# One core: the first batch's attention heads multiply P with v in 64 columns, and their x has one half

## The chip, the cores and the metric

The kernel runs on one core of one Trainium2 chip. The metric is the device time of one execution in microseconds (us), lower is better. Before the change it is 1084.87 us, the median of three runs (1084.13 to 1085.30).

## The reference, cut to what matters

Four batches of eight attention heads (sequence 576, head dimension 64, a mask of 64-row blocks) give x; x passes a dense layer pair with a product, and then a router and eight experts of which each token uses two.

```python
scores = scale * np.matmul(q, k.transpose(0, 1, 3, 2))     # 4 x 8 heads, 576 x 576
attn = np.exp(scores - max); attn = attn / (sum + 1e-09)    # after the mask
x = np.matmul(attn, v)                                       # -> (2304, 512)
a, b = x @ w1, x @ w2
x = (a * b @ w3) @ w_out
...                                                          # router, top 2 of 8 experts
out[mask] += w * (np.maximum(x[mask] @ w1[e], 0.0) @ w2[e])
```

## The kernel before, in words

**Precision.** Products that need more than one pass split a float32 operand into a rounded high part and a low remainder (`split`, L473 to 481: ScalarE writes the high part, VectorE or GpSimd subtracts). `mm3` (L483 to 488) then issues three matmuls, high by high, high by low, low by high. Every expert and dense product goes through L486, L487, L488.

**Attention, heads 8 to 31.** The transposed probabilities P and v are split. The stationary operand `vv` (L619 to 625) is 128 columns wide: 64 of the high part of v, 64 of the low part. P's two parts are multiplied with it in two matmuls. The result has 128 rows, two halves of 64 whose sum is the head's output. Both halves are written to the DRAM tensor `x2[head, 128, 576]` and added later.

**Attention, heads 0 to 7 (the first batch).** P and v stay plain float32, one matmul per piece (the trace shows two records for each). v is loaded into columns 0 to 63 of a 128-column tile `vz` (two tiles, filled with zeros once at L590 to 593, loaded at L600 to 605). So rows 64 to 127 of the result are zeros. They are copied out of PSUM, written to `x2`, read back and added like the others.

**Matmul pieces of one head.** `av_a` (L685) multiplies the last piece, 128 columns of P, into a bank of the pool `tp`, and VectorE copies it into `ev` (L692). `av_b` (L694) does five pieces of 448, 448, 320, 192 and 128 columns in two steps, three pieces and then two. ScalarE copies the result into `ev` (L705), and the SyncE (SP) queue writes `ev` to `x2` (L706).

**The dense layers.** x is consumed in nine chunks of 256 tokens (`Moe1.steps`). Chunks 0 and 1 lie in the first batch (tokens 0 to 511); of chunk 2, 64 tokens do; chunks 3 to 8 need none of it. For a chunk, `x_load` reads both halves of `x2` into `x.ab` and the reciprocal row sums into `x.r`, all on SP. `x_prep` has three steps: GpSimd adds the two halves (L191), VectorE multiplies by the reciprocal sums (L194), and `split` gives the two parts `xh` (L477, L481). Chunk 0 is taken in two parts of three and one tile (heads 0 to 5, then 6 and 7), the others in one.

**The order of work.** Each attention head is a list of short operations written out by hand (`FIRST` for heads up to 9, `LATER` after). `f2.9` in it lets a generator put about 2.9 us of other TensorE work there: first the product of w3 and w_out (`w_unit`, L722), then the dense layers. `c` feeds the conversion of weights: 1024-column pieces come as 64-bit integers (L540), VectorE turns them into float32 in three passes (L549, L550, L551) and `split` makes the parts `pc` (L477, L481). An `ahead` step places `x_load` and the three steps of `x_prep`. When the program is built, each engine's final order is made from these lists, their priorities and a simulated timeline. Each engine then works its own list in order, and SP issues almost every plain DMA, also in order.

**Names in the rows.** `sb` are banks of scores (L644 to 647), `pb` is exp (L663), `tp` L677 the transposes of P, `pt` P transposed (L681, L683), `av` L702 and `tp` L690 the products of P and v, `hi` and `kl` the parts of q and k (L612 to 617), `stg` and `stf` raw and converted weights, `pc` their parts, `m<-xh` the dense products, L711 a transpose of the sums with 40 columns.

Of the kernel before, what the change touches and what calls it, by code (L numbers as in the profile page):

```python
# [8 lines left out]
F32 = mybir.dt.float32  # L9
# [5 lines left out]
OP = mybir.AluOpType  # L15
# [4 lines left out]
B, H, S, D = 4, 8, 576, 64  # L20
NT, DM, DF, E = 2304, 512, 1024, 8
BH = B * H
P = 128
# [6 lines left out]
CH = 256  # L30
# [17 lines left out]
AV0 = 1280  # L48
# [33 lines left out]
class Moe1:  # L82
# [72 lines left out]
    def x_load(self, c):  # L155
        nc, k, p2 = self.nc, self.k, self.p2
        x = self.xs[c] = Ctx()
        x.ab = self.p2b.tile([P, 4, 2, CH], F32, name="xab")
        x.r = self.p2b.tile([P, 4, CH], F32, name="xr")
        t0, o = c * CH, 0  # L160
        while o < CH:
            b, s = divmod(t0 + o, S)
            n = min(CH - o, S - s)
            for g, e in self.parts(c):
                for hh in range(2):
                    hs = slice(hh * 64, (hh + 1) * 64)
                    for ab in range(2):
                        d = nc.sync.dma_start(x.ab[hs, g:e, ab, o:o + n],
                                              k.x2[b * H + 2 * g:b * H + 2 * e, ab * 64:(ab + 1) * 64, s:s + n]
                                              .rearrange("(t q) d s -> q d t s", q=2)[hh])  # L170
                        for h in range(b * H + 2 * e, (b + 1) * H):
                            self.tc.declare_no_dep(d.ins, k.x2w[h].ins, reason="another head")
                    nc.sync.dma_start(x.r[hs, g:e, o:o + n],
                                      k.rs[b, 2 * g:2 * e, s:s + n].rearrange("(t q) s -> q t s", q=2)[hh:hh + 1]
                                      .broadcast_to([64, e - g, n]))
            o += n
        if ZC <= c < ZC + 4:
            with self.tc.issue_after(d.ins):
                self.setup_dram(c - ZC + 1)
# [6 lines left out]
    def x_prep(self, c, step):  # L186
        nc, p2 = self.nc, self.p2
        x = self.xs[c]
        if step == 0:
            for g, e in self.parts(c):  # L190
                nc.gpsimd.tensor_tensor(x.ab[:, g:e, 0, :], x.ab[:, g:e, 0, :], x.ab[:, g:e, 1, :], op=OP.add)  # L191
        elif step == 1:
            for g, e in self.parts(c):
                nc.vector.tensor_tensor(x.r[:, g:e, :], x.ab[:, g:e, 0, :], x.r[:, g:e, :], op=OP.mult)  # L194
        else:
            x.h = self.p2b.tile([P, 2, 4, CH], F32R, name="xh")
            for g, e in self.parts(c):
                self.k.split((x.h[:, 0, g:e], x.h[:, 1, g:e]), x.r[:, g:e, :])
# [266 lines left out]
class Kernel:  # L465
# [89 lines left out]
    def attention(self):  # L555
        tc, nc, a = self.tc, self.nc, self.a
        moe1 = self.moe1
        stgs = ExitStack()
        with tc.tile_pool(name="p1", bufs=1, side="right") as p1, \
# [15 lines left out]
            px = moe1.px = pxs.enter_context(tc.tile_pool(name="px", bufs=1))  # L575

            def buf(h, shape, dt, name):

                return (px if h < H and h % 2 else p1).tile(shape, dt, name=name)
# [7 lines left out]

            vz = []  # L590
            for h in range(2):
                vz.append(px.tile([P, 5, P], F32, name=f"vz{h}"))
                nc.gpsimd.memset(vz[h], 0.0)

            def load(h):
                c = hd[h] = Ctx()
                c.qk = buf(h, [P, 2, S], F32, "qk")
                nc.sync.dma_start(c.qk, a["qk"][h])

            def load_v(h):  # L600
                c = hd[h]
                if h < H:
                    c.vv = vz[h % 2]
                    nc.sync.dma_start(c.vv[:, :, 0:D], a["v"][h])
                    return
                c.v = p1.tile([P, 5, D], F32, name="v")
                nc.sync.dma_start(c.v, a["v"][h])
# [77 lines left out]
            def av_a(h):  # L685
                c = hd[h]
                bank = psT.tile([P, 512], F32, name="tp")
                m = c.pt.shape[1]
                for i in range(m):
                    nc.tensor.matmul(bank[:, 0:P], c.vv[:, 0, :], c.pt[:, i, AV0:AV0 + P], start=(i == 0), stop=(i == m - 1))  # L690
                c.ev = buf(h, [P, S], F32, "ev")
                nc.vector.tensor_copy(c.ev[:, 0:128], bank[:, 0:128])  # L692

            def av_b(h, kts):  # L694
                c = hd[h]
                if kts[0] == 0:
                    c.av = psV.tile([P, 512], F32, name="av")
                for kt in kts:
                    _, s0, w, o0 = AV_UNITS[kt]
                    m = c.pt.shape[1]  # L700
                    for i in range(m):
                        nc.tensor.matmul(c.av[:, o0:o0 + w], c.vv[:, kt, :], c.pt[:, i, s0:s0 + w],  # L702
                                         start=(kt == 0 and i == 0), stop=(kt == 4 and i == m - 1))
                if kts[-1] == 4:
                    nc.scalar.copy(c.ev[:, 128:576], c.av[:, 0:448])  # L705
                    self.x2w[h] = nc.sync.dma_start(self.x2[h], c.ev)  # L706

            def sums_out(b):
                sp = psT.tile([P, 512], F32, name="tp")
# [113 lines left out]
            prep_h(0)  # L823
            load(1)
            load_v(0)
            feed()
            feed()

            def step(i, j, op):
# [4 lines left out]
                elif kind == "c":  # L834
                    feed()
                elif kind == "t":
                    tick()
                elif kind == "g" and i >= 0:
                    g_unit(i, int(n))
                elif kind == "p" and i >= 0:  # L840
                    prep_v(i)
                elif kind == "a" and i >= 0:
                    av_a(i)
                elif kind == "b" and i >= 0:
                    av_b(i, [0, 1, 2] if n == "0" else [3, 4])
                elif kind == "s" and j < BH:
                    s_unit(j, int(n))
                    s_max(j)
                elif kind == "h" and j + 1 < BH:
                    prep_h(j + 1)  # L850
                elif kind == "v" and 0 < j < BH:
                    load_v(j)
                elif kind == "l" and j + 2 < BH:
                    load(j + 2)
                elif kind == "o":
                    if i == H - 1 or i > H and i % H == 0:
                        sums_out((i - 1) // H if i > H else 0)
                    if i >= H:
                        moe1.ready = i // H
                    if i == 12:  # L860
                        assert not moe1.scat
                        with tc.issue_after(self.x2w[i - 1].ins):
                            moe1.setup_dram(0)
# [259 lines left out]
```

## Time and profile before

| | |
|---|---|
| Median of three runs | 1084.87 us (1084.13 to 1085.30) |
| The profiled execution | 1085.58 us |
| Its span, first to last instruction | 1083.8 us |
| Granted TensorE clock, mean | 0.987 of 2.4 GHz |
| TensorE matmul / VectorE / ScalarE / GpSimd busy | 1041.4 / 563.9 / 495.2 / 302.8 us |
| Attention of the first batch | about 10 to 110 us |
| Attention of the other batches, with the dense layers between | about 110 to 462 us |
| Dense layers' end and the experts | to 1083.8 us |

PE is TensorE's matmul side, PEld its weight loads, DVE VectorE, ACT ScalarE, POOL GpSimd, SP SyncE's queue. In a timeline row the first number is the start in us from the span's start, the second the stretch of time that the merged instructions cover, and what stands in brackets is how long the engine had been idle and what released it. Matmuls overlap in the pipe, so the distance from one start to the next tells what a matmul costs, not the length of its record. In a table by stretch each engine has its busy us and its number of instructions, then the granted clock, the share of time that the DMA engines were busy, and GB/s.

### The profile page before, as it was taken

The numbers are of one execution on the slowest core, as the hardware profiler recorded it, in microseconds if no ns is written. First come the engines' busy times: TensorE is split into PE (matmuls) and PEld (weight loads), VectorE is DVE, ScalarE is ACT, GpSimd is POOL, SyncE is SP. The second block draws the span as 40 slices with busy tenths as digits, with TensorE's granted clock in tenths as the row PEclk, the third lists the DMA queues.
The fourth block names the chain that finished last, engine by engine and source line by source line (L and its number), as shares of the span: only waits on it lengthen the run. The fifth ranks groups of instructions, "written<-read, shape, count | busy, mean of one in ns | idle before, by whom it ended". The sixth has DMA issues, their size and how long they took to land.

```text
span 1083.8 us, 17396 instructions
## 1 busy us (share of the span) xinstructions
PE 1041.4 (96%) x6588; PEld 941.8 (87%) x6588; DVE 563.9 (52%) x1211; ACT 495.2 (46%) x1163; POOL 302.8 (28%) x306
## 2 busy tenths in 40 slices
PE   6999887999999999999999999999999999999996
PEld 4777776899998989999999889889898989999885
DVE  7988898676764757443345443533333333434110
ACT  6875466566665666422223432533333333434111
POOL 2000233225252424332444224241413132220211
PEclk9999898999999999999999999999999999999998
DMA  8764878235653363222413355663535445351312
GB/s 269 255 225 152 222 206 170 82 108 134 184 118 104 122 186 98 78 80 59 79 45 114 98 125 170 183 158 98 153 101 147 108 129 125 108 117 31 39 20 32
DMA packets 78962, 136.34 MB, mean 126 GB/s; under 512 B 21165, under 2 KB 46485, under 8 KB 77717
## 3 DMA queue, kind: packets, MB, share of 16 engines
q1 hardware_dynamic: 68757, 113.98, 35.9%
q0 software_dynamic: 10112, 21.16, 10.7%
q8 instruction: 54, 0.88, 0.3%
q14 instruction: 39, 0.32, 0.1%
HBM read 103.92 MB, written 31.19 MB: 125 GB/s over the span
## 4 chain that ended last, share of the span: by engine, by line
PE 78%; DVE 3%; DMA 2%; ACT 1%; issue 1%; SPq 0%; POOL 0%; POOLq 0%; ACTq 0%; DVEq 0%
PE ph L486 13%; PE ph L488 13%; PE ph L487 13%; PE m L486 9%; PE m L487 9%; PE m L488 9%; PE tp L677 3%; PE av L702 3%; PE sb L647 1%; PE sb L644 1%; PE m L955 1%; DMA stf<-in_m_dram 1%; DMA yt<-cst 1%; PE m L244 1%; DVE pc L481 1%; PE m L235 1%
## 5 line engine op out<-in xcount | busy, mean ns | idle before, releaser
L486 PE MATMUL m<-xh,pc 128*128 128x256 f32 x576 | 166.9, 292 | 4.3 <-DVE pc L481 3.0
L487 PE MATMUL m<-xh,pc 128*128 128x256 f32 x576 | 163.7, 288 | 0.0
L488 PE MATMUL m<-xh,pc 128*128 128x256 f32 x576 | 162.3, 288 | 0.4 <-DVE pc L481 0.3
L486 PE MATMUL ph<-xt,pc 128*128 128x384 f32 (+1 forms) x512 | 156.1, 308 | 3.5 <-DVE ht L970 1.9
L487 PE MATMUL ph<-xt,pc 128*128 128x384 f32 (+1 forms) x512 | 157.1, 307 | 0.0
L488 PE MATMUL ph<-xt,pc 128*128 128x384 f32 (+1 forms) x512 | 156.9, 307 | 0.0
L970 DVE SCALAR_TENSOR_TENSOR ht<-ph,ht 128x384 fp32r<-128x384 f32 (+1 forms) x128 | 62.0, 490 | 148.8 <-ACT ht L969 142.9
L481 DVE TENSOR_TENSOR pc<-stf,pc 128x1024 fp32r<-128x1024 f32 (+1 forms) x75 | 88.1, 1190 | 87.9 <-ACT pc L477 83.8
L486 PE MATMUL ph<-pc,ht 128*128 128x512 f32 x320 | 126.0, 395 | 0.0
L488 PE MATMUL ph<-pc,ht 128*128 128x512 f32 x320 | 124.6, 390 | 0.0
L487 PE MATMUL ph<-pc,ht 128*128 128x512 f32 x320 | 124.5, 390 | 0.0
L997 POOL DMA_INDIRECT out_dram<-yo,ids x40 | 66.1, 1651 | 209.1 <-ACT yo L993 107.9
L969 ACT ACTIVATE ht<-ph 128x384 fp32r<-128x384 f32 (+1 forms) x128 | 55.1, 438 | 135.0 <-PE ph L488 132.5
L486 PEld LDWEIGHTS m<-xh,pc 128*128 128x128 f32 x576 | 111.3, 194 | 5.6 <-DVE pc L481 3.2
L487 PEld LDWEIGHTS m<-xh,pc 128*128 128x128 f32 x576 | 110.9, 194 | 0.8 <-DVE xh L481 0.2
L481 POOL TENSOR_TENSOR gt<-at,gt 128x256 fp32r<-128x256 f32 x72 | 59.2, 826 | 187.2 <-ACT gt L477 168.9
L488 PEld LDWEIGHTS m<-xh,pc 128*128 128x128 f32 x576 | 110.3, 194 | 1.0 <-DVE pc L481 0.8
L663 ACT ACTIVATE pb<-sb,nm 128x320 f32<-128x320 f32 (+3 forms) x192 | 93.7, 498 | 23.3 <-PE tp L677 15.5
L486 PEld LDWEIGHTS ph<-xt,pc 128*128 128x128 f32 x512 | 95.8, 188 | 4.5 <-DVE ht L970 2.1
L477 ACT CAST pc<-stf 128x1024 fp32r<-128x1024 f32 (+1 forms) x75 | 74.8, 1016 | 54.0 <-DMA stf<-in_m_dram 32.8
L487 PEld LDWEIGHTS ph<-xt,pc 128*128 128x128 f32 x512 | 96.1, 188 | 0.5 <-DVE xt L481 0.2
L488 PEld LDWEIGHTS ph<-xt,pc 128*128 128x128 f32 x512 | 96.2, 188 | 0.0
(159 smaller groups left out, 2164.4 us busy)
## 6 DMA issues: line engine op xcount, KB each, us to landing
stf<-in_m_dram SPq DMA_DIRECT2D x52, 512.0 KB
qk<-in_qk_dram SPq DMA_DIRECT2D x32, 576.0 KB
stg<-in_w_dram SPq DMA_DIRECT2D x14, 1024.0 KB
x<-ev SPq DMA_DIRECT2D x32, 288.0 KB
xab<-x SPq DMA_DIRECT2D x20, 256.0 KB
yt<-y SPq DMA_DIRECT2D x18, 260.0 KB
v<-in_v_dram SPq DMA_DIRECT2D x24, 160.0 KB
out_dram<-cst SPq DMA_DIRECT2D x3, 1280.0 KB
```

Of the source, the lines that this page charges most:

```text
L235: nc.tensor.transpose(px[:, d, :], y[:, d * P:(d + 1) * P], self.k.ident)
L477: d = nc.scalar.copy(h, src)
L481: return d, eng.tensor_tensor(l, src, r32(h), op=OP.subtract)
L486: nc.tensor.matmul(out, a, c, start=first, stop=False)
L487: nc.tensor.matmul(out, a, d, start=False, stop=False)
L488: nc.tensor.matmul(out, b, c, start=False, stop=last)
L663: nc.scalar.activation(pb[t][:, k0:k0 + src.free_size()], src, AF.Exp, bias=nm, scale=1.0, accum_out=sums[:, h // H, t + n, h % H:h % H + 1])
L677: nc.tensor.transpose(bank[:, n * P:(n + 1) * P], pb[t][:, kt * P:(kt + 1) * P], self.ident)
L702: nc.tensor.matmul(c.av[:, o0:o0 + w], c.vv[:, kt, :], c.pt[:, i, s0:s0 + w], start=(kt == 0 and i == 0), stop=(kt == 4 and i == m - 1))
L969: a = nc.scalar.activation(hh[:, 0, f, :], ph, AF.Relu)
L970: v = nc.vector.scalar_tensor_tensor(hh[:, 1, f, :], ph, 0.0, r32(hh[:, 0, f, :]), op0=OP.max, op1=OP.subtract)
L997: nc.gpsimd.indirect_dma_start(out=self.a["out"], out_offset=self.idx(e, i), in_=yo, in_offset=None, compute_op=OP.add)
```

## The change

v of the first batch is loaded into a 64-column tile and used as it is, so its matmuls have 64 stationary columns and 64 result rows. `av_a` and `av_b` take the number of rows from the tile (`r`, `c.vv.shape[2]`), the copies out of PSUM and the write to `x2` have 64 rows for those heads and 128 for the others. `x_load` reads one half for tokens of the first batch. The GpSimd add is skipped for chunks 0 and 1, done for the last 192 tokens of chunk 2, and for all of chunks 3 to 8. The two `vz` tiles and their fills go.

```diff
                 for hh in range(2):
                     hs = slice(hh * 64, (hh + 1) * 64)
-                    for ab in range(2):
+                    for ab in range(2 if b else 1):
                         d = nc.sync.dma_start(x.ab[hs, g:e, ab, o:o + n],
...
         if step == 0:
-            for g, e in self.parts(c):
-                nc.gpsimd.tensor_tensor(x.ab[:, g:e, 0, :], x.ab[:, g:e, 0, :], x.ab[:, g:e, 1, :], op=OP.add)
+            o = min(max(S - c * CH, 0), CH)
+            if o < CH:
+                xa, xb = x.ab[:, :, 0, o:], x.ab[:, :, 1, o:]
+                nc.gpsimd.tensor_tensor(xa, xa, xb, op=OP.add)
...
-            vz = []
-            for h in range(2):
-                vz.append(px.tile([P, 5, P], F32, name=f"vz{h}"))
-                nc.gpsimd.memset(vz[h], 0.0)
...
                 if h < H:
-                    c.vv = vz[h % 2]
-                    nc.sync.dma_start(c.vv[:, :, 0:D], a["v"][h])
+                    c.vv = px.tile([P, 5, D], F32, name="vz", bufs=2)
+                    nc.sync.dma_start(c.vv, a["v"][h])
                     return
...
                 bank = psT.tile([P, 512], F32, name="tp")
-                m = c.pt.shape[1]
+                m, r = c.pt.shape[1], c.vv.shape[2]
                 for i in range(m):
-                    nc.tensor.matmul(bank[:, 0:P], c.vv[:, 0, :], c.pt[:, i, AV0:AV0 + P], start=(i == 0), stop=(i == m - 1))
-                c.ev = buf(h, [P, S], F32, "ev")
-                nc.vector.tensor_copy(c.ev[:, 0:128], bank[:, 0:128])
+                    nc.tensor.matmul(bank[0:r, 0:P], c.vv[:, 0, :], c.pt[:, i, AV0:AV0 + P], start=(i == 0), stop=(i == m - 1))
+                c.ev = buf(h, [P, S], F32, "ev")[0:r, :]
+                nc.vector.tensor_copy(c.ev[:, 0:128], bank[0:r, 0:128])
...
-                    c.av = psV.tile([P, 512], F32, name="av")
+                    c.av = psV.tile([P, 512], F32, name="av")[0:c.vv.shape[2], :]
...
-                    self.x2w[h] = nc.sync.dma_start(self.x2[h], c.ev)
+                    self.x2w[h] = nc.sync.dma_start(self.x2[h, 0:c.vv.shape[2], :], c.ev)
```

## Rows read from the trace of the kernel before

**Rows 1.** The page: busy time of the engines.

```profile
PE 1041.4 (96%) x6588; PEld 941.8 (87%) x6588; DVE 563.9 (52%) x1211; ACT 495.2 (46%) x1163; POOL 302.8 (28%) x306
```

**Rows 2.** Table by stretch: the stages.

```profile
80.00:110.00 30.00, 30.00 (x157) 23.86 (x156) 26.61 (x37) 16.33 (x38) 1.87 (x1) 1.00 0.48 162
...
120.00:140.00 20.00, 16.50 (x100) 14.75 (x100) 16.37 (x25) 8.16 (x19) 5.79 (x4) 0.83 0.77 209
...
160.00:200.00 40.00, 32.84 (x203) 28.77 (x204) 36.66 (x56) 24.75 (x67) 13.09 (x10) 0.87 0.66 153
200.00:300.00 100.00, 99.74 (x725) 92.30 (x724) 66.28 (x188) 63.97 (x184) 32.35 (x31) 1.00 0.47 130
```

**Rows 3.** The chain that ended last, 170 to 200 us.

```profile
188.11 1.49 DVE pc L481
...
198.00 0.38 PE m L488
```

**Rows 4.** Groups by line and shape: count, busy us, mean ns, idle before.

```profile
L690 PE MATMUL tp<-pt,vz 128*128 128x128 f32 x16 | 3.1, 277 | 0.0
...
L711 PE MATMUL tp<-ident,sums 128*40 128x128 f32 x4 | 1.1, 272 | 0.3 <-DVE pt L683 0.3
...
L191 POOL TENSOR_TENSOR xab<-xab 128x1024 f32<-128x1024 f32 x8 | 19.1, 2388 | 0.0
```

**Rows 5.** PE's timeline, 87.5 to 89 us.

```profile
87.86 0.71 PE L702 MATMUL av<-pt,vz 128*128 128x192 f32 x4
88.40 0.49 PE L677 MATMUL tp<-ident,pb 128*128 128x128 f32 x3
```

**Rows 6.** PE's timeline, 99 to 99.6 us.

```profile
99.14 0.40 PE L488 MATMUL m<-pc,pc 128*128 128x512 f32 x1
99.38 0.27 PE L711 MATMUL tp<-ident,sums 128*40 128x128 f32 x1
99.49 0.54 PE L702 MATMUL av<-pt,vz 128*128 128x448 f32 x1
```

**Rows 7.** SP's waits, 0 to 120 us: total us, times, longest.

```profile
SPq L540 <- DVE stf L551: 38.0, 10, 7.0
```

**Rows 8.** Line L168's issues on SP: ns least, median, most; first and last start.

```profile
L168 SPq DMA_DIRECT2D xab<-x x52: 573/608/1157, 110.5 to 523.6; - x52
```

**Rows 9.** Table by stretch: around chunk 0's arrival.

```profile
110.00:125.00 15.00, 14.47 (x78) 11.95 (x76) 11.95 (x18) 7.65 (x19) 2.11 (x2) 1.00 0.93 250
...
129.30:134.50 5.20, 5.20 (x24) 5.01 (x25) 3.64 (x8) 1.72 (x6) 0.00 (x0) 0.50 0.96 267
```

**Rows 10.** POOL's timeline, 108 to 160 us.

```profile
119.72 1.84 POOL L191 TENSOR_TENSOR xab<-xab 128x768 f32<-128x768 f32 x1 [14.49 <-DMA xr<-rs]
124.72 0.89 POOL L191 TENSOR_TENSOR xab<-xab 128x256 f32<-128x256 f32 x1 [3.17 <-DMA xab<-x]
```

**Rows 11.** DVE's timeline, 108 to 160 us.

```profile
121.59 0.96 DVE L194 TENSOR_TENSOR xr<-xab,xr 128x768 f32<-128x768 f32 x1 [1.90 <-POOL xab L191]
...
126.61 1.62 DVE L194 TENSOR_TENSOR xr<-xab,xr 128x256 f32<-128x256 f32 x1
...
133.64 0.56 DVE L658 TENSOR_REDUCE nm<-sb 128x1 f32<-128x128 f32 x2 [1.20 <-PE sb L647]
134.84 0.49 DVE L658 TENSOR_REDUCE nm<-sb 128x1 f32<-128x320 f32 x1 [0.64 <-PE sb L647]
```

**Rows 12.** PE's timeline, 125.9 to 129.7 us.

```profile
129.26 0.58 PE L486 MATMUL m<-xh,pc 128*128 128x256 f32 x1 [2.97 <-DVE pc L481]
```

**Rows 13.** POOL's timeline, 140 to 300 us.

```profile
184.95 2.36 POOL L191 TENSOR_TENSOR xab<-xab 128x1024 f32<-128x1024 f32 x1
```

**Rows 14.** DVE's timeline, 184 to 198 us.

```profile
185.40 2.52 DVE L614 SCALAR_TENSOR_TENSOR hi<-qk,hi 64x576 fp32r<-64x576 f32 x1 [0.63 <-ACT hi L612]
```

**Rows 15.** Line L614 on DVE, all heads: ns least, median, most.

```profile
L614 DVE SCALAR_TENSOR_TENSOR hi<-qk,hi x32: 755/756/2723, 6.9 to 432.0; 64x576 fp32r<-64x576 f32 x32
```

**Rows 16.** PE's timeline, 187 to 188.3 us.

```profile
188.07 0.33 PE L644 MATMUL sb<-hi 128*128 128x192 f32 x1 [2.21 <-DVE hi L614]
```

## The prediction, made before the changed kernel was run

> **What bounds the kernel now.** I read the page's busy times first. PE is busy for 96% of the span [rows 1], so the question is where it is not, and whose work it then waits for. The table by stretch answers that [rows 2]. From 80 to 110 us, in the first batch's attention, PE is busy all of the 30 us. From 200 us on it is again (99.74 of 100). Between 120 and 200 us it is not: 16.50 of 20 and 32.84 of 40 us, at a mean granted clock of 0.83 and 0.87. In the same stretches DVE is busy for 16.37 of 20 and 36.66 of 40. So there are two regimes. From 200 us on, the time is PE's list, and work that starts earlier there ends the kernel earlier by as much. From 120 to 200 us DVE holds PE up: the chain that ended last runs through DVE's weight conversion at 188.11 and reaches PE at 198.00 [rows 3]. A change can gain in two ways: by shortening PE's list, or by letting DVE get through the stretch from 120 to 200 us sooner.
>
> **The change part by part.**
>
> *Matmuls with 64 columns.* The count stays, and so do the moving columns. Four records of the first batch's products (two of 192 columns, two of 128, 640 in all) take from 87.86 to 88.40, 0.54 us or 0.84 ns a column [rows 5]. The time goes with the moving columns, which the change leaves alone, so a shorter weight load beside them frees nothing: 0. Could narrow columns cost something? The trace has one such matmul, L711 with 40 columns, four times [rows 4]. Its start lies 0.24 us behind a 512-column matmul's, and the next, 128 columns wide, starts 0.11 us behind it [rows 6]. So 0 is taken from the nearest row. The upper bound is the record's 0.277 us less the 0.11 us from start to start, 0.17 us at each change of width, if the pipe had to empty there. I put no gain below nothing, since the same columns stream.
>
> By the Trainium skill, page "TensorEngine Tiling (Array Packing)", section "Key Properties", changing the tiling mode drains TensorE. If 64 result columns counted as such a mode, the sum would lose that bound at each border. Row L711 shows no drain for 40 columns; no run here shows 64.
>
> *Loads of v, fills, copies, writes to x2.* The write of a head to x2 halves, and v arrives in rows five times as long. Until 120 us SP's weight loads L540 wait 38.0 us in total for DVE to free a buffer [rows 7], so the pace there is DVE's and not a transfer's: 0. The fills stand at the start on POOL, of whose time the stretch from 80 to 110 us uses 1.87 us [rows 2]; 0. The copies L692 and L705 keep their columns and lose only partitions; 0. If that cover went, an issue of about 0.6 us on SP [rows 8] would be the most that one load could move. Edits with one answer: nothing together, at most 1 us either way.
>
> *Chunk 0's loads.* Eight issues of `xab` become four. At a median of 0.608 us [rows 8] SP is through 2.4 us earlier, 1.2 us of it before the first part's last read. The bytes fall by 2 x 64 rows x 4 tiles x 256 x 4 B = 524 KB. At the 250 GB/s of 110 to 125 us, when the DMA engines were busy 0.93 of the time [rows 9], that is 2.1 us. So the first part, which released POOL at 119.72, lands about 2 us earlier. By itself this is worth nothing, since DVE is at other work until then; it makes sure that the next term is had in full. The weight loads behind it in SP's list also go out sooner, but they wait for DVE's buffers anyway.
>
> *Chunk 0's add.* It goes: 1.84 us for three tiles, 0.89 us for one [rows 10]. DVE sat idle 1.90 us for the first of these, until 121.59 [rows 11]. With the data there, this idle time goes: **-1.9 us**. The second add hides behind DVE's conversion (DVE had no wait before 126.61), 0. What is late next is PE's work: it stood still for 2.97 us until 129.26, for a DVE subtraction that comes after both multiplications in DVE's list [rows 12]. With 1.9 us off in front of it, about 1 us of that remains. After the standstill PE ran at half clock, 0.50, for the 5.20 us from 129.30 [rows 9], and DVE in turn waited 1.20 and 0.64 us for scores [rows 11]. A standstill a third as long should not bring the clock down for so long, and the scores then come before DVE asks: **-1.84 us**. Between no gain and all of PE's standstill plus half of the slow stretch (2.97 + 2.60 = 5.6 us) I take DVE's two waits, since DVE is the bound.
>
> *One more bound here.* The second multiplication took 1.62 us for 256 columns, when 768 took 0.96 [rows 11]. In proportion it would be 0.3. POOL's subtraction for a head ran beside it and stays, only a little earlier. So 0, with -1.3 us as the end of the range.
>
> *Chunk 1's add.* It ran on POOL from 184.95 for 2.36 us [rows 13]. Beside it DVE's L614 began at 185.40 and took 2.52 us [rows 14], against a median of 0.756 over 32 heads [rows 15], and PE stood 2.21 us for it [rows 16]. It ended 0.6 us after the add, as if it had waited for POOL. The add gone, L614 takes its median: 2.52 - 0.76 = **-1.76 us**. This lies on the path, 0.2 us before the chain's conversion step at 188.11 [rows 3]. If another POOL operation moves into its place, the gain is 0.
>
> *Chunk 2.* Its add falls from 1024 to 768 elements. By the 2388 ns of the others [rows 4] and the 1.84 us of chunk 0's, that is 0.55 us of POOL, in the stretch from 200 us on in which PE is full [rows 2]: 0.
>
> **Sum:** 1.9 + 1.84 + 1.76 = 5.5 us. The profiled execution took 1085.58 us with a span of 1083.8; the sum makes it 1080.1. The median of the runs is 0.71 us below that execution, so I predict **1079.4 us**.
>
> **The rivals.**
>
> *Small gain.* DVE's work itself shrinks nowhere; only its waits and collisions do. If they come back elsewhere, say because POOL's other subtractions now meet DVE's work at other places, one of the three terms is left: 1.8 to 1.9 us, so about 1083.0. For it speaks DVE's 36.66 of 40 us [rows 2]; against it that all three waits have their releaser named in the rows.
>
> *Slower, by draining.* Each border between 64 and 128 columns empties PE's pipe. The hand-written list has three places per head (`b0`, `a`, `b1`), so 3 x 8 heads x 2 borders = 48. At 0.17 us each this is 8.2 us in a stretch where PE is full: 1084.87 - 5.5 + 8.2 = 1087.6. It decides from about 0.16 us a border, since 5.5 + 2.2 us must be outweighed. Against it speaks L711 [rows 6].
>
> By the same page and section of the Trainium skill it is this rival that would come true; by that rule, the trace does not agree as far as 40 columns show.
>
> *Slower, by order.* Each engine's order comes from a simulated timeline. If chunk 1's multiplication and split, ready earlier without the add, are set ahead of a weight conversion on DVE, PE waits longer for its weights. By chunk 0's multiplications that is 0.96 + 1.62 = 2.6 us, and as much again if the clock halves afterwards as at 129.30, against the gain of 1.76 us that is left: 1084.87 - 1.76 + 5.2 = 1088.3. It decides where the move stands before a conversion that PE awaits. Nothing in the rows speaks for it but that DVE is full.
>
> *Nothing.* If the second half still had to be waited for, or the first part's wait was for the sums (the profile names `xr<-rs` as POOL's releaser), 1084.9.
>
> **How the numbers follow.** About 0.2% (2.2 us) is what a measurement of this kernel can tell from no change. Chances: the forecast (gains from 3.5 us up) 0.58; small gain 0.24, half of it over 2.2 us; draining 0.05; order 0.08; nothing 0.05. So faster 0.58 + 0.12 = 0.70, same 0.12 + 0.05 = 0.17, slower 0.13. The range goes from 1075.0 to 1085.0. Its low end adds to the forecast the 1.3 us of the slow multiplication and PE's part that I did not take (5.6 - 1.84, rounded down to 3). Its high end takes in the small gain and no change; both slower rivals and larger gains stay outside.
>
> **What would show it.** Right, step by step: no L191 before chunk 2's, and seven L191 in place of ten; DVE's first L194 without a wait; PE's standstill before the second dense product under 1.5 us and no 5 us at 0.50 after it; L614 of that head near 0.76 us; first-batch products still at 0.84 ns a column. Wrong: gaps at each border of narrow matmuls; an L614 or L481 on DVE at 2 us and more beside another POOL operation; or PE's standstills moved to later conversions between 140 and 200 us, with the sum of its idle time there as before.

## The result, and the profile after

The changed kernel is slower. Its median is 1098.68 us (1096.03 to 1100.64, 4 runs) against 1084.50 us (1083.79 to 1085.30, 4 runs) of the kernel before: ratio 1.0128, 95% interval 1.0112 to 1.0145. The prediction was 1079.4 us, in a range from 1075.0 to 1085.0. The profiled execution took 1100.64 us with a span of 1098.8; the one of before took 1085.58. So these two executions differ by 15.1 us.

The page of the changed kernel gives the busy times of the engines:

```profile
PE 1051.3 (96%) x6588; PEld 934.9 (85%) x6588; DVE 560.7 (51%) x1211; ACT 493.1 (45%) x1163; POOL 290.7 (26%) x301
```

PE issues as many instructions as before and is busy 9.9 us longer [rows 1]. The table by stretch (columns as in rows 2):

```profile
80.00:110.00 30.00, 30.00 (x146) 20.58 (x147) 25.56 (x40) 16.12 (x38) 1.56 (x1) 1.00 0.51 171
120.00:140.00 20.00, 20.00 (x122) 17.32 (x121) 18.33 (x29) 11.18 (x28) 2.77 (x2) 1.00 0.74 211
160.00:200.00 40.00, 26.39 (x177) 22.27 (x175) 30.72 (x50) 20.76 (x57) 7.09 (x6) 0.87 0.66 164
200.00:300.00 100.00, 95.35 (x658) 84.73 (x658) 65.69 (x150) 60.40 (x171) 32.67 (x30) 1.00 0.42 118
```

Against rows 2 there are four things to see. In 80 to 110 us PE is busy all the time, as before, but does 146 instructions instead of 157: the same "full" engine does less. In 120 to 140 us the hole is gone (20.00 of 20, clock 1.00). In 160 to 200 us PE lost 6.5 us (26.39 against 32.84). And after 200 us, where PE was full, 4.4 us are missing (95.35 against 99.74).

To see when the time goes, I added up the moving columns of all matmuls in each trace, in order of time. Those of plain float32 products and transposes, at 0.84 ns a column, count twice those of the others, at 0.45. The lag at a moment t is by how much later the other trace reaches the sum that the kernel before has at t. The sums at the end are the same in all traces, but the order of the work differs somewhat, so a lag is good to about 1 us. All are against the one trace of the kernel before, also for runs on other chips. In microseconds, for the changed kernel and the experiments:

```
t of before         20    80   120   140   180   190   210   260   300   500
after              0.3   6.6   8.5   4.0  -0.4   6.5   9.7  10.3  14.9  16.7
e1_pad128         -0.2   0.6   0.5  -3.9  -7.2  -9.8  -6.4  -4.8  -5.0  -4.6
e2_narrow_only     0.6   7.2  10.7   7.8   1.9  10.5  17.2  17.2  23.0  23.4
e3_zero14         -0.9   6.6   8.4   4.1  -1.8  -4.3   0.3   0.4   4.3   5.0
e4_before_zero14  -0.2   0.4   0.3   0.9   0.9  -0.2   1.0   0.8   0.8   0.8
e5_zero14_zc4      0.3   7.9   9.7   5.2  -0.7  -3.2   0.2   0.3   0.5   2.5
e6_pad72           0.4   0.3   0.3  -2.0  -3.4  -3.8  -3.4  -1.9  -1.9  -0.1
e7_half            1.1   4.5   5.9   2.2   0.8   0.8   2.1   3.7   3.6   3.9
e8_pad_zero14     -0.1   0.4   0.2  -4.6  -7.0  -9.6  -8.1  -6.6  -6.8  -4.9
e9_cols40          0.5   4.0   6.5   3.0   3.0   1.2   1.7   3.2   3.1   3.4
```

The row "after" tells four stories. The kernel loses 8 us in the first 120 us, most of it by 80. It wins 9 back by 180 us. It loses 10 between 180 and 210 us, and 4.6 more between 260 and 300. The 9 us won back can't be put down to the missing adds: e2, which keeps them, wins 8.8 back in the same stretch. What the missing half and adds are worth is read from e1, which works in the order of the kernel before up to about 117 us.

**The first loss: TensorE stops at each border.** The narrow matmuls have the form 128*64 now. These are their groups (columns as in rows 4; the last two lines are weight loads, theirs and those of the kernel before):

```profile
L699 PE MATMUL av<-pt,vz 128*64 128x448 f32 x32 | 15.5, 565 | 0.0
L699 PE MATMUL av<-pt,vz 128*64 128x192 f32 x16 | 4.3, 348 | 0.0
L687 PE MATMUL tp<-pt,vz 128*64 128x128 f32 x16 | 3.5, 298 | 0.0
L699 PEld LDWEIGHTS av<-pt,vz 128*64 128x64 f32 x80 | 8.8, 136 | 5.2 <-issue 4.3
...
L702 PEld LDWEIGHTS av<-pt,vz 128*128 128x128 f32 x80 | 12.9, 194 | 0.6
```

A weight load is shorter (136 ns, 194 before), with half the columns. But the unit that loads weights stands idle ahead of them for 5.2 us in all, 0.6 before, and for 4.3 of the 5.2 by "issue": for nothing that the profile shows. The records themselves hardly grow (L687 298 ns, 277 before [rows 4]), so the totals of the page hide the cost. PE's timeline around the 40-column transpose shows it, start and duration in us; it is the place of rows 6. First the kernel before, from that transpose on, PE and then its weight loads:

```profile
99.49 0.92 PE L702 MATMUL av<-pt,vz 128*128 128x448 f32 x2
100.24 0.27 PE L677 MATMUL tp<-ident,pb 128*128 128x128 f32 x1
...
99.38 0.30 PEld L702 LDWEIGHTS av<-pt,vz 128*128 128x128 f32 x2
```

Then the changed kernel:

```profile
93.23 0.27 PE L708 MATMUL tp<-ident,sums 128*40 128x128 f32 x1
93.44 0.96 PE L699 MATMUL av<-pt,vz 128*64 128x448 f32 x2
94.33 0.50 PE L490 MATMUL m<-pc,pc 128*128 128x512 f32 x1
...
93.00 0.10 PEld L708 LDWEIGHTS tp<-ident,sums 128*40 128x40 f32 x1
93.43 0.19 PEld L699 LDWEIGHTS av<-pt,vz 128*64 128x64 f32 x2 [0.33 <-issue]
94.33 0.19 PEld L490 LDWEIGHTS m<-pc,pc 128*128 128x128 f32 x1 [0.70 <-issue]
```

Before, the weights of the product were loaded at 99.38, while the transpose streamed (its start is 99.38 too), and the product started 0.11 us behind the transpose. Now the load waits until 93.43, and product and load start together, 0.20 us behind it. At the way out the same: the load for L490 starts at 94.33, with the matmul that needs it. From the transpose's start to the start of what follows the two products it was 0.86 us (99.38 to 100.24) and is 1.10 us. So a run of narrow matmuls, one border in and one out, costs about 0.24 us (0.235 unrounded). The trace's order of PE has 31 such runs: 31 x 0.235 = 7.3 us, against 8.2 us of lag gained from 20 to 120 us. All but the first of the 31 look alike: beyond the streaming of the columns, at 0.844 ns each, the way out takes 0.14 to 0.15 us more, and the way in behind a transpose 0.095 us, where nothing was left over between 128-column products and transposes before. A run of eight records pays no more than one of two. In this stretch all of it counts, since PE is the bound there.

By the Trainium skill, page "TensorEngine Tiling (Array Packing)", section "Key Properties", changing the tiling mode drains TensorE, and its section "Tiling Modes" lists 128x64 as a mode of its own. The trace agrees for these 64 columns, with 0.24 us a run.

**The gain came.** DVE's timeline has chunk 0's two multiplications with no idle time ahead of them, and no add on POOL before chunk 2:

```profile
114.52 0.96 DVE L196 TENSOR_TENSOR xr<-xab,xr 128x768 f32<-128x768 f32 x1
...
120.83 0.41 DVE L196 TENSOR_TENSOR xr<-xab,xr 128x256 f32<-128x256 f32 x1
```

**The second and third loss: loads of v behind other transfers.** PE's timeline, then ScalarE's, have one long wait each before 192 us; the number in brackets is the idle time and what ended it. The third line is ScalarE's in the kernel before:

```profile
192.04 0.69 PE L674 MATMUL tp<-ident,pb 128*128 128x128 f32 x2 [8.27 <-ACT pb L660]
...
191.04 0.46 ACT L621 CAST vv<-v 128x320 fp32r<-128x320 f32 x1 [8.89 <-DMA v<-in_v_dram]
...
188.72 0.46 ACT L624 CAST vv<-v 128x320 fp32r<-128x320 f32 x1 [1.42 <-DMA v<-in_v_dram]
```

ScalarE's list is in order: the split of v (L621) stands in it ahead of the exponentials that PE waits for (L660). In the kernel before, the same split waited 1.42 us, in this one 8.89. The issues on SP, start and duration, show why. Before:

```profile
170.12 0.55 SPq L540 DMA_DIRECT2D stg<-in_w_dram  x1
170.88 0.46 SPq L706 DMA_DIRECT2D x<-ev  x1
...
176.95 0.46 SPq L147 DMA_DIRECT2D yt<-cst  x1
177.46 2.79 SPq L149 DMA_DIRECT2D yt<-cst  x2
180.35 0.97 SPq L607 DMA_DIRECT2D v<-in_v_dram  x1
```

And after:

```profile
171.16 0.33 SPq L703 DMA_DIRECT2D x<-ev  x1
...
175.49 0.55 SPq L542 DMA_DIRECT2D stg<-in_w_dram  x1
176.09 0.62 SPq L147 DMA_DIRECT2D yt<-cst  x1
176.75 6.75 SPq L149 DMA_DIRECT2D yt<-cst  x2
183.60 1.14 SPq L604 DMA_DIRECT2D v<-in_v_dram  x1
```

The zero writes to the y table (L147, L149) are placed behind head 11's write to `x2` (L706, now L703), whatever else SP has just issued. Now 1 MB of weights was issued directly ahead of them, the two zero writes took SP 6.75 us instead of 2.79, and v went out 3.2 us later, behind 1 MB of weights and 0.79 MB of zeros. It arrived at about 191. From 186 to 189 us PE did nothing, while the DMA engines moved 343 GB/s; at that rate the 1.8 MB alone take about 5.3 us:

```profile
186.00:189.00 3.00, 0.00 (x0) 0.00 (x0) 0.69 (x1) 0.00 (x0) 0.00 (x0) 0.50 1.11 343
```

What differs is SP's list, not the time at which the heads arrive. Head 11's write goes out at 171.16 us against 170.88, and the lag at 180 us is -0.4. But in the list of the kernel before that weight load stands ahead of head 11's write, and in the changed kernel behind it, between the index tables and the zeros. The list is made when the program is built. All four kernels here without the fills and the padded tiles (after, e2, e3, e5) have the last two weight loads behind twelve writes of `x2`; all nine with them, whatever the width of their matmuls, behind eleven.

With the second set of zero writes, which has 1.3 MB of zeros for the output in it, PE stops again. The chain that ended last (start, duration):

```profile
287.15 2.09 SPq L703
289.35 1.07 SPq L595
290.52 6.35 DMA v<-in_v_dram
```

The last of the zero writes was issued by 287.1 there. PE was busy for 6.5 of the 9 us from 292 to 301 and then ran from 301 to 304 at a granted clock of 0.50. A write of `x2` stood behind the zeros as well, and DVE waited for it:

```profile
295.14 0.29 DVE L689 COPY ev<-tp 128x128 f32<-128x128 f32 x1 [1.57 <-DMA x<-ev]
```

In the kernel before, the second set was issued by 273.4, 6 us ahead of the next load of v (279.39). That distance alone doesn't decide it: in e1 it is 3.3 us, here 3.4, and e1's lag doesn't grow there.

### The profile page after: what moved, and what is told of

Its sections match the earlier page's. It is cut to its first block, busy times and chain, and to the rows that moved or that the text cites. A ratio compares the mean times of both kernels' runs of the same rounds, so it can differ in the third digit from the quotient of the medians.

```text
span 1098.8 us, 17377 instructions
## 1 busy us (share of the span) xinstructions
PE 1051.3 (96%) x6588; PEld 934.9 (85%) x6588; DVE 560.7 (51%) x1211; ACT 493.1 (45%) x1163; POOL 290.7 (26%) x301
## 4 chain that ended last, share of the span: by engine, by line
PE 75%; DVE 2%; DMA 2%; ACT 1%; issue 1%; SPq 1%; POOL 0%; POOLq 0%; ACTq 0%; DVEq 0%
PE ph L488 13%; PE ph L489 13%; PE ph L490 13%; PE m L488 9%; PE m L490 9%; PE m L489 9%; PE tp L674 2%; PE av L699 2%; PE m L952 1%; PE sb L644 1%; PE sb L641 1%; DMA stf<-in_m_dram 1%; PE m L246 1%; PE m L237 1%; DMA v<-in_v_dram 1%
## 5 line engine op out<-in xcount | busy, mean ns | idle before, releaser
L490 PE MATMUL m<-xh,pc 128*128 128x256 f32 x576 | 163.1, 289 | 0.1
L490 PE MATMUL ph<-xt,pc 128*128 128x384 f32 (+1 forms) x512 | 156.9, 307 | 0.0
L483 DVE TENSOR_TENSOR pc<-stf,pc 128x1024 fp32r<-128x1024 f32 (+1 forms) x75 | 88.6, 1197 | 87.5 <-ACT pc L479 83.5
L490 PE MATMUL ph<-pc,ht 128*128 128x512 f32 x320 | 124.6, 390 | 0.0
L490 PEld LDWEIGHTS m<-xh,pc 128*128 128x128 f32 x576 | 110.1, 194 | 0.5 <-DVE pc L483 0.3
L660 ACT ACTIVATE pb<-sb,nm 128x288 f32<-128x288 f32 (+3 forms) x192 | 93.5, 498 | 27.4 <-PE tp L674 17.9
L488 PEld LDWEIGHTS ph<-xt,pc 128*128 128x128 f32 x512 | 95.8, 188 | 3.5 <-ACT xt L479 2.1
L489 PEld LDWEIGHTS ph<-xt,pc 128*128 128x128 f32 x512 | 96.1, 188 | 0.5 <-DVE xt L483 0.2
L655 DVE TENSOR_REDUCE nm<-sb 128x1 f32<-128x128 f32 (+2 forms) x192 | 78.7, 438 | 34.9 <-PE sb L644 34.1
```

What stands on the lines that cost most here:

```text
L483: return d, eng.tensor_tensor(l, src, r32(h), op=OP.subtract)
L488: nc.tensor.matmul(out, a, c, start=first, stop=False)
L489: nc.tensor.matmul(out, a, d, start=False, stop=False)
L490: nc.tensor.matmul(out, b, c, start=False, stop=last)
L655: nc.vector.tensor_reduce(nm[:, n:n + 1], o[:, 0:w], axis=AX, op=OP.max, negate=True)
L660: nc.scalar.activation(pb[t][:, k0:k0 + src.free_size()], src, AF.Exp, bias=nm, scale=1.0, accum_out=sums[:, h // H, t + n, h % H:h % H + 1])
```

## The experiments

The theory: A, borders of narrow matmuls; B, loads of v that meet the zero writes, because the heads stand at another point of SP's list. (The expectations take B as a matter of the heads' time; the two SP lists above show it as one of the list.) Rivals: the other order of work that the planner makes without the add (C), and, for A, anything else about 64 columns (the layout of v, the copies and writes of 64 rows).

**e1_pad128: the gain alone.** v again in the padded tiles of before, the rest as in the changed kernel (`q` is 64 in the first batch, 128 after it):

```diff
-                    c.vv = px.tile([P, 5, D], F32, name="vz", bufs=2)
-                    nc.sync.dma_start(c.vv, a["v"][h])
+                    c.vv = vz[h % 2]
+                    nc.sync.dma_start(c.vv[:, :, 0:D], a["v"][h])
...
-                c.ev = buf(h, [P, S], F32, "ev")[0:r, :]
+                c.ev = buf(h, [P, S], F32, "ev")[0:q, :]
```

> The changed kernel, with v of the first batch in tiles of 128 columns padded with zeros as before, so that the matmuls are 128 columns wide; x still has one half and chunks 0 and 1 their missing adds. Theory A (each run of 64-column matmuls costs 0.235 us of PE in and out; 31 runs in the trace after): 7.3 us come back at least in the first 120 us, where the heads' x writes should stand within 1 us of the kernel before instead of 8 later. What follows depends on theory B (the 8.3 us stall at 183 to 192 us and the 4.6 us at 292 to 304 us are v loads caught behind the zero writes of the y table, because the heads stand at another point of the queue): if the heads stand about where they did before, both stalls are gone too and the time is the 1084.5 of before less the 5.5 of the missing adds, 1078 to 1081; if the stalls stay, 1091. Rival C (the other order of work that the planner makes once the add is gone costs by itself, whatever the width): 1095 to 1099.

Measured: 1081.0 us against 1086.29 of the kernel before on the same chip, ratio 0.9960 (0.9939 to 0.9982). The lag at 120 us is 0.5, and both stalls are gone, but for a wait of 2.6 us on ScalarE for v at 185 us (1.42 before). C falls as I put it: the planner without the add is 0.4% faster than before. So the loss comes with the 64-column tile. That isn't yet the 64 columns alone, since e1 also has the fills again, and in SP's list the last weight loads ahead of head 11's write, as in the kernel before. The timelines of DVE, PE, POOL and SP in this run have the prediction's steps:

```profile
118.53 0.96 DVE L196 TENSOR_TENSOR xr<-xab,xr 128x768 f32<-128x768 f32 x1 [2.55 <-DMA xr<-rs]
...
127.74 0.38 PE L488 MATMUL m<-xh,pc 128*128 128x256 f32 x1 [1.44 <-DVE pc L483]
...
180.91 1.80 DVE L616 SCALAR_TENSOR_TENSOR hi<-qk,hi 64x576 fp32r<-64x576 f32 x1
...
180.68 1.42 POOL L619 TENSOR_TENSOR kl<-qk,hi 128x576 fp32r<-128x576 f32 x1 [1.20 <-ACT hi L617]
...
182.86 0.33 PE L646 MATMUL sb<-hi 128*128 128x192 f32 x1 [0.30 <-DVE hi L616]
...
175.73 1.02 SPq L149 DMA_DIRECT2D yt<-cst  x2
176.84 0.62 SPq L609 DMA_DIRECT2D v<-in_v_dram  x1
```

And the table by stretch, behind PE's standstill:

```profile
130.00:134.50 4.50, 4.50 (x38) 4.23 (x37) 4.47 (x8) 1.87 (x6) 0.00 (x0) 1.00 1.02 269
```

PE's standstill for chunk 0 is 1.44 us (2.97 before [rows 12]) and no stretch at half clock follows (1.00). DVE still waits 2.55 us, but for the sums (`rs`), 3.06 us earlier than before, 118.53 against 121.59 [rows 11]. The zero writes here take 1.02 us; the weights had been issued 9.3 us ahead of them, at 166.47. With 7.3 us between (the kernel before) they take 2.79, with 1.3 us (the changed kernel) 6.75.

**e2_narrow_only: the narrow matmuls alone**, put into the kernel before; `ev` of the first batch has 64 rows:

```diff
-                    self.x2w[h] = nc.sync.dma_start(self.x2[h], c.ev)
+                    if h < H:
+                        self.x2w[h] = nc.sync.dma_start(self.x2[h].rearrange("(a p) s -> p a s", a=2), c.ev.unsqueeze(1).broadcast_to([D, 2, S]))
+                    else:
+                        self.x2w[h] = nc.sync.dma_start(self.x2[h], c.ev)
```

> The kernel before, with v of the first batch as loaded and 64-column matmuls alone; each head's 64 rows are written to both halves of x2, and the adds stay (x of the first batch comes out doubled). Theory A: the first 120 us lag by 7 to 8 us, so 1084.5 + 7.3 = 1092, and up to 1100 if the v loads then meet the zero writes (B). If narrow matmuls cost nothing, 1084 to 1085. The second multiplication of chunk 0 and the 1.9 and 1.8 us waits for the add are to be seen as before.

Measured: 1105.24 us, ratio 1.0166 (1.0146 to 1.0185). The lag at 120 us is 10.7, somewhat over A's 8, and ScalarE then waits 10.5 us for a load of v; the second stall adds 5.8 us by 300. That is more than the 1100 that I gave as the most. Between 120 and 180 us the lag falls from 10.7 to 1.9 with all the adds in place.

**e3_zero14 and e4_before_zero14: the first zero writes two heads later**, in the changed kernel and in the kernel before:

```diff
-                    if i == 12:
+                    if i == 14:
```

> The changed kernel, with the writes of index tables and zeros to the y table issued two heads later (at head 14, not 12). Theory B: the stall of 8.3 us on TensorE at 183 to 192 us goes, with the 3 us of waits behind it at 200 to 210 us; 1098.7 - 8 to 10 = 1089 to 1091, unless the writes collide with a later v load in the same way, which would show as a stall of 5 to 8 us some 20 to 25 us later and leave 1095 to 1099. Theory A alone (all 14 us are borders): 1098 to 1099, the stall moved but without effect. The lag of 8 us at 120 us stays by both.

> The kernel before, with the same move of the writes of index tables and zeros from head 12 to head 14. It is the control of e3: the kernel before has a stall of only 1.4 us on ScalarE for v there. Theory B: 1081 to 1086 where no v load is caught, up to 1092 where one is. If the move by itself saved several us here as well, what e3 gains would not be the undoing of the change's collision.

Measured: e3 1090.45 us, ratio 1.0040 (1.0027 to 1.0054); e4 1084.4 us, 0.9976 (0.9960 to 0.9992). In e3 the lag at 210 us is 0.3 instead of 9.7: the first stall costs over 9 us with the refilling behind it. B is right that it is the meeting with the zero writes; why they meet is read from SP's list, above. The lag at 120 us is the same 8.4. The control moved by less than 3 us, and its trace runs level with the kernel before. So e3's gain is an undone collision and not a better place in general.

**e5_zero14_zc4: both sets later.**

```diff
-ZC, NF = 3, 10
+ZC, NF = 4, 10
...
-                    if i == 12:
+                    if i == 14:
```

> The changed kernel with both sets of zero writes moved: the first to head 14 (as in e3_zero14), the second from chunk 3 to chunk 4. Theory B: in e3_zero14 the lag behind the kernel before went from +0.3 us at 260 us to +4.3 at 300, where the second set still meets a v load; without that meeting the lag stays near 0 to the end, 1090.45 - 4.3 = about 1086, level with the kernel before (the borders' 8 us against the 5.5 us of the adds and a little else). If the second stall has another cause, 1090 as e3_zero14; if the second set meets another v load, 1090 with a stall some 20 us later.

Measured: 1089.06 us against 1090.92, ratio 0.9987 (0.9968 to 1.0005). The lag no longer grows between 260 and 300 us (0.3 to 0.5; e3 0.4 to 4.3). The table by stretch shows PE full there again, 99.31 of 100:

```profile
200.00:300.00 100.00, 99.31 (x707) 90.77 (x708) 67.38 (x180) 62.27 (x178) 31.14 (x29) 1.00 0.47 110
```

With both collisions gone the changed kernel is level with the one before, by the times on this chip; by the traces it lags by 2.5 us at 500. So the borders take what the missing adds give, or a little more.

**e6_pad72: 72 columns**, 8 of them zeros (the padded tiles of e1 with 72 in place of 128).

> The changed kernel, with v padded with 8 columns of zeros to 72 (matmuls 72 columns wide, of which 64 rows are copied out). It tells narrowing as such from a step at 64 columns. Theory A as I hold it (the hardware goes to a half-width tile at 64 columns and stops at each border): no stop at 72 columns, the lag at 120 us within 1 us of the kernel before as in e1_pad128, time 1079 to 1083. Rival: any matmul narrower than its neighbours stops TensorE: lag of 8 us at 120 us, time 1095 to 1101.

Measured: 1085.52 us against 1090.92, ratio 0.9941 (0.9919 to 0.9962), lag 0.3 at 120 us. There is no stop: in its timeline of PE and of the weight loads, the product starts 0.11 us behind the transpose again, and its weights are loaded meanwhile:

```profile
95.61 0.27 PE L713 MATMUL tp<-ident,sums 128*40 128x128 f32 x1
95.72 0.91 PE L704 MATMUL av<-pt,vz 128*72 128x448 f32 x2
96.47 0.38 PE L679 MATMUL tp<-ident,pb 128*128 128x128 f32 x2
...
95.61 0.25 PEld L704 LDWEIGHTS av<-pt,vz 128*72 128x72 f32 x2
```

So narrowing as such is free; the step lies between 72 and 64. The 0.6% of gain is less sure than that: the lag at 500 us is -0.1, and the kernel before spread over 8 us on this chip.

**e7_half: half of the heads narrow**, from the same padded tiles as e1:

```diff
-                    c.vv = vz[h % 2]
+                    c.vv = vz[h % 2][:, :, 0:D + D * (h % 2)]
```

> e1_pad128 with the even heads of the first batch multiplied by the first 64 columns of the same padded tiles and the odd heads by all 128: half of the runs of narrow matmuls, 14 to 16 instead of 31. Theory A: the lag at 120 us is 14 to 16 x 0.25 = 3.5 to 4 us more than e1_pad128's 0.5. The total depends on where the heads then stand to the zero writes: 1084 to 1085 without a stall, 1089 to 1096 with one or two. If the lag came from the layout of v in SBUF or from the 64-row copies and writes, and not from the borders, the lag at 120 us would be near 0.5 or near 8.

Measured: 1088.39 us against 1090.92, ratio 0.9971 (0.9958 to 0.9985). With 15 runs of narrow matmuls the lag at 120 us is 5.9, of which 1.1 was there at 20 us, ahead of the first of them. So 4.8 us lies between e1's 0.7 and the changed kernel's 8.2, a little above the 3.5 to 4 of theory A. The layout of v and the 64-row copies are those of e1, so they aren't the cause. Nor is the order of work: PE's and SP's lists in e6, e7 and e9 are the same entry by entry, and with 0, 15 and 28 runs of narrow matmuls the lag at 120 us is 0.3, 5.9 and 6.5.

**e9_cols40: why the 40-column transpose had told nothing.** Rows 40 to 63 of `ev` are filled with zeros:

```diff
-                    c.vv = vz[h % 2]
+                    c.vv = vz[h % 2][:, :, 0:40]
```

> e1_pad128 with the first batch's matmuls taking only the first 40 of v's columns; rows 40 to 63 of each head's x are zeros, so a part of x is left out. It asks why the four 40-column transposes, on which the prediction rested, showed no stop. If transposes are exempt and matmuls of 64 columns or fewer all stop TensorE: the entry into a run of these matmuls after a 128-column transpose takes 0.20 us as with 64 columns (0.11 when 128 wide), with the weight load begun only when the transpose is done, and the lag at 120 us is 7 to 10 us. If only widths near 64 stop it and 40 does not, entry 0.11 us and lag under 1 us.

Measured, in a single run: 1088.35 us (the kernel before on this chip 1087.37), lag 6.5 at 120 us, with 28 runs; I had expected 7 to 10. PE's timeline and the weight loads:

```profile
100.65 0.27 PE L716 MATMUL tp<-ident,sums 128*40 128x128 f32 x1
100.85 0.95 PE L706 MATMUL av<-pt,vz 128*40 128x448 f32 x2
...
100.42 0.10 PEld L716 LDWEIGHTS tp<-ident,sums 128*40 128x40 f32 x1
100.85 0.15 PEld L706 LDWEIGHTS av<-pt,vz 128*40 128x40 f32 x2 [0.32 <-issue]
```

The two lines have the same form, 128*40. The transpose's weights are loaded at 100.42, while the matmul before it (it starts at 100.42) streams; the multiplication's weights wait for the transpose to end. A transpose of 40 columns doesn't stop TensorE, a multiplication with 40 does, and even between the two there is a border.

This run also parts the lag from the collision. It comes to 120 us 6 us late, but SP's list is that of e6, and ScalarE hardly waits for v behind the zero writes (e7: 0.98 us):

```profile
192.39 0.46 ACT L626 CAST vv<-v 128x320 fp32r<-128x320 f32 x1 [0.55 <-DMA v<-in_v_dram]
```

**e8_pad_zero14, e8_again and e10_pad_zero14_zc4: a version that beats both.** e1 with `i == 14` for the first zero writes; e10 with `ZC` 4 as well.

> e1_pad128 with the first set of zero writes moved to head 14. It is the candidate for the best version. In e1_pad128 the lag goes from -9.8 us at 190 us to -6.5 at 200 us: if that is the zero writes' meeting with a load, the move keeps up to 3 us more, 1078; otherwise 1081 as e1_pad128. The same move gave the kernel before 0.24%, 2 us, so 1078 to 1079 by that too.

> The candidate once more, beside the kernel before on this chip, in five rounds: padded v, x of one half, first zero writes at head 14. From its traces (-4.5 to -6.7 us against the kernel before) 0.993 to 0.996; its earlier 0.9905 stood against a kernel before that spread over 8 us.

> The candidate with the second set of zero writes moved from chunk 3 to chunk 4 as well. The padded kernels show no lag growing between 260 and 300 us, so nothing is to be had there: within 1 us of e8_again, unless the second set now meets a v load, 3 to 5 us slower.

Measured: e8 1079.89 us against 1090.92, ratio 0.9905 (0.9877 to 0.9932); the same kernel again, 1081.56 against 1087.37, 0.9939 (0.9916 to 0.9962); e10 1081.14, 0.9935 (0.9908 to 0.9962). In e8 the lag goes from -9.6 to -8.1 where e1's goes from -9.8 to -6.4. So the padded kernel gains 0.6% or more on the kernel before; whether the move of the zero writes adds to e1's 0.4% the intervals don't tell, and e10's second move adds nothing that can be measured. On one chip, e5 and e8 differ by 0.9987 - 0.9905, some 9 us: the price of the narrow matmuls when no load collides. By the ratios of e8's repetition, or of e10, which moves the same zero writes as e5, it is 5 to 6 us; by the lags at 500 us it is 7.

## Why the prediction was wrong

**The step that failed** is the first: "*Matmuls with 64 columns* ... So 0 is taken from the nearest row". The nearest row, L711, was no instance of the thing: it is a transpose, and e9 shows that a transpose of 40 columns passes without a stop where a multiplication of 40 stops. The bound that I set beside it, 0.17 us at each change of width, was good: about 0.12 us a border (0.235 a run). The rival priced it at 48 borders and 8.2 us; the trace has 62 and 8 us. That the products agree is luck: too few borders, each too dear. I had given this rival 0.05. Against it stood one row with four records of another operation, and that is no ground for so low a chance. For it stood the rule of the Trainium skill cited there, and with that rule the trace agrees for multiplications with 64 and with 40 columns; at the transposes with 40 no stop is seen.

**The second step that failed** is larger than the first. Both slower rivals ended near 1088, and the kernel took 1098.7. The rest is the two collisions, some 9 and 4.5 us by the lags of e3 and e5, somewhat more than that difference. The term "*Loads of v, fills, copies, writes to x2* ... nothing together, at most 1 us either way" was argued from the first 120 us only, and it was worth some 14 us, mostly at 180 to 210 us. I priced no move of a load against the zero writes at head 12 and chunk 3, although the rival "Slower, by order" says that each engine's order is made anew from a simulated timeline. I looked for that on DVE; it came on SP, where a weight load had passed behind head 11's write. Which part of the change moved it was not run by itself. In these kernels it goes with the missing fills and padded tiles, and not with the width: e9, with fills and 40 columns, has the list of e6. Nor did a run move the weight load and the zero writes apart; e3 moves the zeros away from both.

**Matmuls' rate:** right. 320, 192 and 128 columns keep their durations within about 20 ns, by the records; the cost is between them.

**Chunk 0's loads and add, -3.74 us:** right in size. e1 shows PE's standstill at 1.44 us ("about 1 us remains"; "under 1.5") and no stretch at half clock; its lag falls by 4.4 us from 120 to 140. DVE's wait did not vanish but moved 3 us earlier, to the sums, which the rival "Nothing" had named.

**Chunk 1's add, -1.76 us:** right for the path, wrong by its row. L614 (L616 in e1) did not fall to 0.76 but to 1.80 us, with another subtraction on POOL (1.42 us) beside it, as the step's last sentence feared. PE waits 0.30 us for it in e1 instead of 2.21 [rows 16]. But it then waits 2.5 us for exponentials behind the load of v, and from 180 to 210 us e1's lag rises from -7.2 to -6.4: of this term nothing is left.

**The sum of 5.5 us:** e1, the change without its narrow matmuls, gained 0.4%, 4.3 us (2.0 to 6.6). That this is near the sum is in part luck. By e1's lags 4.4 us come by 140 us, as forecast; 3.3 more come from 140 to 180, for which the sum has no term; and 2.4 go again from 180 to 260, where its third term stood. The 3.3 us were not traced to a cause. The small gain of 1.8 did not come, nor the order rival at the place that it named.

**What I said would show it wrong** did: the gaps at each border are there, as idle time of the weight loads and not of PE, which the page counts as busy.

## What to carry to other kernels

A multiplication with 64 (or 40) stationary columns among wider ones costs a stop at each change, here 0.12 us a border; where TensorE is the bound, pad the columns (72 and 128 were both free) or keep the narrow ones together. Judge a rule of the hardware by a row of the same operation, not by one that only has the same shape. And when each engine's order is made anew with every build, compare the queue's list before and after, entry by entry, around the large transfers that sit at fixed places: look which small load now comes behind them.

## What the hardware showed that I had not expected

A transpose with 40 columns and a multiplication with 40 behave differently at a border (0.11 us in rows 6, e9 0.20 us from the transpose to the multiplication). The time of a stop is charged to nobody: PE's busy share was 30.00 of 30 us with 146 instructions and with 157, and only the idle time "issue" of the weight loads and the starts of neighbouring records show it. And 8 us of lag were made good by 180 us, yet 14 us more were lost behind them. At the first 10 of these the heads were on time; what had changed was the place of one weight load in SP's list.
